# An H3 scan block with a gated linear unit, forward and backward: the first shift's loads, the queue of the h stores, and the transforms of slice 0

## The chip, the cores and the metric

The kernel runs on one core of a Trainium2 chip. The metric is the device time of one execution in microseconds, here the median of eight runs. TensorE (PE) multiplies matrices, VectorE (DVE), ScalarE (ACT) and GpSimd (POOL) work on elements, and SyncE (SP) only issues DMAs; ACT and POOL issue DMAs too. Each engine runs its own list of instructions in order and waits for the others by semaphores.

## The reference

The program computes a block's output and the gradients of its inputs. S is 2048, D is 1024, F is 3584, everything is bf16 at the edges. The core of the forward side:

```python
def _A_ref(q, k, v, shift_k, ssm_k, ssm_D):      # q is the layer-normed x
    k_shift = sum over t of k_pad[:, t:t + S, :] * shift_k[:, ks - 1 - t]     # 4 taps
    kv = k_shift * v
    y = irfft(rfft(kv, padded to 2S) * rfft(ssm_k, padded to 2S))[:S]
    return q * (y + kv * ssm_D)

def _B_ref(x, w_gate, w_up, w_down):
    return ((x @ w_gate) * (x @ w_up)) @ w_down

xn = _layernorm(A_q)
out = A_q + _A_ref(xn, ...) * silu(_B_ref(xn, ...))
```

The shortened sums stand for the padded loops and the einsums of the original. The outputs are `out` and nine gradients from a vjp with a given output gradient.

## The kernel before

The time has five stretches. A layer norm of the 16 blocks of 128 rows comes first (0 to about 57 us). The forward stage (to about 547 us) multiplies the normed rows with 14 slabs of 256 columns of gate and up weights, and beside it runs the long convolution. Then come the product with w_down and the gate (to about 740 us), the backward products with the backward convolution beside them, and last dx with the layer norm's gradient.

A gate/up *unit* is `gu_unit`: four blocks (one or two in the first units) of one slab. Each block is a *group* of eight 128x512 matmuls into `psg` (L622), evicted by ACT to `gut` (L624). After the unit, VectorE multiplies the halves to `hN` (L632), which is stored to Hd by POOL. Five groups later PE transposes hN into a PSUM tile `tr` (L642), ACT copies it to `hT` (L643, two buffers), and it is stored to HTd. Units are counted below in the order of their hN.

The convolution works on slices of 128 channels, two to a `shift`. A shift (L667) forms kv from the shifted k and v with eight VectorE operations over 128x4096 each. Its inputs are k from `KSLd` in two halves and v, all loaded by POOL (`cld`) in `load_kv`, and the taps `Wbc`. A forward transform of kv or of the filter h goes through PE against sine and cosine tables `TF` into `psF` (L234, two PSUM buffers), is copied by ACT to `SP` (L256 or L294, two buffers), and is finished on VectorE. There are two forms. The four-residue form (`fwd4_half`) splits the sequence less on VectorE and multiplies both table halves on PE, 32 matmuls of 128x256; the eight-residue form (`fwd8_half`, `fwd8`) does one more butterfly step on VectorE, 16 matmuls. The list EIGHT says which slices take the second form. After that come the product of the spectra, an inverse transform on VectorE (`inv_dft`) and on PE (`inv_rows`, into `psY`), and `yf`, stored to YFd.

`angles` on POOL makes the integer angles of the tables, `mask_angles` on VectorE reduces them, `build_tables` on ACT takes the sines, `turn_tables` transposes them on PE. `Dz` is a row of ssm_D that enters the h transform by a small matmul (L239).

What sets the order: instructions are recorded in program order and a scheduler places them on the engines. `tc.issue_after(x)` keeps what is inside behind x. Once `PIN[0]` is set, VectorE's operations in `tt` and `stt` keep their program order. `conv` is a generator; each `next` records one piece and yields its weight. `pump` runs it up to a share of its total weight, and `tick`, called after each gate/up group, raises that share. `st` issues on POOL, `ld` on SP, `sta` on ACT. In the first stretch the loop over `xs` records the layer norms and first units, and inside it the pieces of set-up work, among them `next(conv)`, which loads one half of k and v.

Of the kernel before, what the change touches and what calls it, by code (L numbers as in the profile page):

```python
# [10 lines left out]
ACT = mybir.ActivationFunctionType  # L11
# [8 lines left out]
def build_kernel(  # L20
# [11 lines left out]
    nc = tc.nc  # L32
    P = 128
    _, S, D = A_q.shape
# [5 lines left out]
    SLW = 256  # L40
    NSL = F // SLW
    EPS = 1e-5
    WSC = 2.0 / 2048.0
# [14 lines left out]
    ADD, SUB, MUL = ALU.add, ALU.subtract, ALU.mult  # L58

    def ld(out, in_):  # L60
        return nc.sync.dma_start(out=out, in_=in_)
# [3 lines left out]
    def st(out, in_):  # L65
        ins = nc.gpsimd.dma_start(out=out, in_=in_)
        if PINQ[0]:
            tc.keep_in_program_order(ins)
        return ins
# [41 lines left out]
    HTd = [[dram.tile([n, S // 2], BF16, name=f"HTd{i}{n}") for n in (24 * P, 4 * P)] for i in range(2)]  # L111
# [43 lines left out]
    def angles(tg):  # L155

        E = nc.gpsimd
        tcol = tg.tile([P, 8], I32, name="tcol")
        E.iota(tcol[:], pattern=[[1, 8]], base=0, channel_multiplier=8)
        f2 = tg.tile([P, P], I32, name="f2")  # L160
        E.iota(f2[:], pattern=[[4, P]], base=1, channel_multiplier=0)
        m = tg.tile([P, 8, P], I32, name="m")
        ins = E.tensor_tensor(m[:], f2[:].unsqueeze(1).to_broadcast([P, 8, P]),
                              tcol[:].unsqueeze(2).to_broadcast([P, 8, P]), ALU.mult)
        mm = tg.tile([P, 8, P], I32, name="mm1")
        E.iota(mm[:], pattern=[[512, 8], [0, P]], base=0, channel_multiplier=0)
        E.tensor_tensor(mm[:], m[:], mm[:], ADD)
        return (m, mm), ins

    def mask_angles(ang):  # L170

        for x in ang:
            V.tensor_single_scalar(x[:], x[:], 4095, ALU.bitwise_and)

# [10 lines left out]
    def turn_tables(psp):  # L185

        for j in range(2):
            for rq in range(2):
                ps = psp.tile([P, 4, 2, P], BF16, name="psY")
                for i in range(4):  # L190
                    for k in range(2):
                        nc.tensor.transpose(ps[:, i, k, :], T4[j][:, 4 * rq + i, k, :], ident[:])
                nc.scalar.copy(out=TI[:, j, 4 * rq:4 * rq + 4], in_=ps[:])
                yield
# [16 lines left out]
    def tt(o, a, b, op):  # L211
        pinned(V.tensor_tensor(o, a, b, op))  # L212
# [306 lines left out]
    Dz = kst.tile([P, D], BF16, name="Dz")  # L519
# [17 lines left out]
    tr_ln, act_copy = [None], [None]  # L537
# [56 lines left out]
    nop = lambda: None  # L594
# [3 lines left out]
    def defer(fn):  # L598
        later.append([0, fn])
# [10 lines left out]
    def gu_unit(sl, b0, n, w, tick):  # L610

        if n == 4:
            gut = fg.tile([P, 2, 4, SLW], BF16, name="gut")
            hN = fg.tile([P, 4, SLW], BF16, name="hN", bufs=3)
        else:
            gut = lnp.tile([P, 2, 2, SLW], BF16, name="gut_s", bufs=6)
            hN = lnp.tile([P, 2, SLW], BF16, name="hN_s", bufs=6)
        for i in range(n):
            q, qi = divmod(b0 + i, 4)
            ps = ps_gu.tile([P, 512], F32, name="psg")  # L620
            for dc in range(DC):
                gu_mm[0] = nc.tensor.matmul(ps[:], XNT[q][:, dc, qi * P:(qi + 1) * P],  # L622
                                            w[:, dc].rearrange("p a f -> p (a f)"), start=(dc == 0), stop=(dc == DC - 1))
            nc.scalar.copy(out=gut[:, :, i], in_=ps[:].rearrange("p (a f) -> p a f", a=2))  # L624
            flush(5)
            hn[0]()
            hn[0] = nop
            tick()
        sta(GUd[sl, b0 // 8][:, :, b0 % 8:b0 % 8 + n], gut[:, :, 0:n])

        def multiply():
            tt(hN[:, 0:n], gut[:, 0, 0:n], gut[:, 1, 0:n], MUL)  # L632
            st(Hd[sl][:, b0:b0 + n, :], hN[:, 0:n])
            defer(turn)
        hn[0] = multiply

        def turn():
            hT = fg.tile([P, 2, 4, P], BF16, name="hT")
            ps = ps_tr.tile([P, 2, 4, P], BF16, name="tr")
            for a in range(2):  # L640
                for i in range(n):
                    nc.tensor.transpose(ps[:, a, i, :], hN[:, i, a * P:(a + 1) * P], ident[:])  # L642
            nc.scalar.copy(out=hT[:, :, 0:n], in_=ps[:, :, 0:n])  # L643
            fr, so = sl % 12 * SLW, b0 % 8 * P
            st(HTd[b0 // 8][sl // 12][fr:fr + SLW, so:so + n * P].rearrange("(a f) s -> f a s", f=P),
               hT[:, :, 0:n].rearrange("f a i s -> f a (i s)"))

    h_out = []
    EIGHT = (7,)
    SHIFT_W = 8 * 2.3  # L650

    def conv_forward():
# [33 lines left out]
        def h_rows(ds):  # L686
            hrow = S_.pop(("h", ds))
            hx = cs.tile([P, NB, P], BF16, name="hx")
            pe_us[0] += 0.95
            for c in range(2):  # L690
                ps = ps_tr.tile([P, 8, P], BF16, name="tr")
                with tc.issue_after(tr_ln[0].ins):
                    nc.tensor.transpose(ps[:, 0, :], hrow[:, c, :, 0], ident[:])
                for r in range(1, 8):
                    nc.tensor.transpose(ps[:, r, :], hrow[:, c, :, r], ident[:])
                nc.scalar.activation(hx[:, 8 * c:8 * c + 8, :], ps[:], ACT.Copy, scale=WSC)
            h_out.append(ds)
            if ds + 1 < 8:
                load_h(ds + 1)
            S_["hx"] = hx  # L700
# [24 lines left out]
        def half(ds, x, i, first=None):  # L725
            if ds not in EIGHT:
                return fwd4_half(x, i, cs, ps_cv, first)
# [4 lines left out]
        def transform(ds, sp, X, C, ahead, step):  # L732

            if ds in EIGHT:
                W = fwd4_buf(cs)[:].rearrange("p a b c x -> p (a b c) x")
# [20 lines left out]

        yield from shift(0)
        PIN[0] = True
        yield 4.0
        h_rows(0)  # L760
        tl = turn_tables(ps_y)
        sp = [half(0, kvs(0), i) for i in range(2)]
        for ds in range(8):
            yield 0.5
            if ds % 2 == 1 and ds < 7:
                with tc.issue_after(S_["kst"].ins):
                    for c in range(2):
# [8 lines left out]
            next(tl, None)  # L776
            room = cs.tile([P, 4, 256], F32, name="room", tag="hx")[:] if ds in EIGHT else None
            yield from transform(ds, sph, HX, room, lambda i: h_rows(ds + 1) if i == 1 and ds < 7 and ds not in EIGHT else None,
                                 lambda: next(tl, None))
            if ds < 7 and ds in EIGHT:  # L780
                h_rows(ds + 1)
# [15 lines left out]
        for _ in tl:  # L797
# [5 lines left out]
    F_TOTAL = 4 * SHIFT_W + 6.0 + 8 * (0.5 + FWD4_W + 1.3 + PROD_W + INV_W) + 10.0 - 0.95 * 8 * (4 * 1.75 + 0.95 + 4 * 0.9)  # L803
    F_TOTAL += len(EIGHT) * 2 * (FWD8_W - 9.6 + 0.95 * 1.75) - 2.0
    conv = conv_forward()
    chunks = [(0, 1), (1, 1), (2, 2), (4, 4), (8, 4), (12, 4)]
    xs = [(b0, n, u8((4, 6, 7)[b0 // 4 - 1], a=4) if n == 4 else lnp.tile([P, n, D], BF16, name=f"x{b0}")[:])
          for (b0, n) in chunks]
    for c in xs[0:2]:
        ln_load(*c)  # L810
    slabs = [load_slab(0, nc.sync)[0]]
# [9 lines left out]
    ang, ang_ins = angles(tg)  # L821
# [4 lines left out]
    last, root, xst = layer_norm(*xs[0])  # L826
    xsts = [xst]
    for i, (b0, n, x4) in enumerate(xs):
        if i + 1 < len(xs):
            with tc.issue_after(last.ins):  # L830
                last, root, xst = layer_norm(*xs[i + 1])
            xsts.append(xst)
        if i == 1:
            with tc.issue_after(xsts[-1].ins):
                for j in range(4):
                    turn_taps(j)
                nc.gpsimd.tensor_single_scalar(Dz[0:1, :], Dz[0:1, :], WSC, MUL)
            with tc.issue_after(last.ins):
                mask_angles(ang)
        if i == 2:  # L840
            with tc.issue_after(xsts[-1].ins):
                spread_taps()
        if i in (3, 4):
            with tc.issue_after(xsts[4].ins):
                next(conv)
        for i_, sl in ([(0, 0)], [(1, 0), (0, 1), (1, 1)], [(2, 0), (2, 1)], [(3, 0), (3, 1)], [(4, 0)], [(5, 0)])[i]:
            gu_unit(sl, *xs[i_][0:2], slabs[sl], nop)
        if i == len(xs) - 1:
            with tc.issue_after(root.ins):
                build_tables(tg, ang)  # L850
    st(RSd.rearrange("(c u r) -> u c r", c=2, u=P), RSTD[:].rearrange("u (c r) -> u c r", c=2))
    st(RSTN[:], RSd.rearrange("(b p) -> p b", p=P))
# [2 lines left out]
    ps_st.release()  # L855
    ps_cv = pool("ps_cv", 2, space=PSUM)
    pump, drain = make_pump(conv, F_TOTAL)
    cnt = [0]
    NT = 24 * 8.0 + 4

    def tick():
        cnt[0] += 1
        pump((SHIFT_W + (F_TOTAL - SHIFT_W) * (cnt[0] + 5) / (NT + 2)) / F_TOTAL)

    pump(SHIFT_W / F_TOTAL)
    for i_, t_ in ((4, nop), (5, tick)):
        gu_unit(1, *xs[i_][0:2], slabs[1], t_)
    for sl in range(2, NSL - 2):
        w, wld = load_slab(sl, nc.sync)
        if sl in (2, 4, 6):  # L870
# [5 lines left out]
    slabs = [load_slab(NSL - 2, nc.sync)[0]]  # L876
# [678 lines left out]
```

## Time and profile before

| | us |
|---|---|
| median of 8 runs (1956.44 to 1966.72) | 1958.92 |
| the profiled execution | 1958.46 |
| its span, first to last instruction | 1956.7 |
| PE busy | 1919.2 |
| VectorE busy | 1518.9 |
| ACT busy | 637.6 |
| POOL busy | 358.7 |
| mean granted TensorE clock | 0.997 |

Busy time is the union of an engine's instructions; what is missing to the span is time in which it stood still. Line numbers (L622) are those of the kernel before. A timeline row has the start in us from the span's start, the length in us, the engine, the line, the operation, the tiles written and read, the shape, the count of merged instructions, and in brackets the idle time before it and what ended that. L212 is the helper `tt`, L66 is `st` and L61 is `ld`, so their rows are told apart by their tiles. A tile name such as U stands for several buffers.

### The profile page before, as it was taken

To read this page: it belongs to the slowest core of one execution; us is meant where nothing else is said; L and a number is where in the kernel's file an instruction comes from. 1 tells how busy PE (TensorE), PEld (TensorE's weight loads), DVE (VectorE), ACT (ScalarE), POOL (GpSimd) and SP (SyncE) were. 2 spreads that over 40 slices of the span, in tenths; PEclk is the share of its full clock that TensorE was granted. 3 is DMA by queue.
4 is the path that set the end of the run, shared out by engine and by line. 5 is a ranking of instruction groups with operands and counts; after the bars stand their busy time and mean duration, and the time that the engine had idled before them with its cause. 6 is when DMAs were issued, how large, how long until landed. Compare 5 with 4: busy or idle time off the path is not lost. (4 is left out here: it accounts for less than half of the span.)

```text
span 1956.7 us, 27285 instructions
## 1 busy us (share of the span) xinstructions
PE 1919.2 (98%) x10909; PEld 1040.6 (53%) x11043; DVE 1518.9 (78%) x1674; ACT 637.6 (33%) x940; POOL 358.7 (18%) x516
## 2 busy tenths in 40 slices
PE   8899999999999999999999999999999999999999
PEld 4555555555444446666566666664444444444444
DVE  8799999899726555888799899999996403778663
ACT  4755555555432224333222222222222102011122
POOL 6222212111112221000113122021121101112111
PEclk8999999999999999999999999999999999999999
DMA  8767757647799989556778779666796999898993
GB/s 280 256 236 268 260 206 248 231 179 233 269 286 304 279 267 325 183 202 214 247 245 269 264 225 277 206 240 217 195 270 161 164 211 213 142 212 168 181 222 116
DMA packets 445279, 448.62 MB, mean 229 GB/s; under 512 B 265876, under 2 KB 362200, under 8 KB 430688
## 3 DMA queue, kind: packets, MB, share of 16 engines
q1 hardware_dynamic: 384832, 232.86, 45.9%
q0 software_dynamic: 44000, 184.65, 28.5%
q10 hardware_dynamic: 16320, 29.36, 4.1%
q8 instruction: 86, 1.41, 0.3%
q14 instruction: 41, 0.34, 0.1%
HBM read 198.20 MB, written 189.84 MB: 198 GB/s over the span
## 5 line engine op out<-in xcount | busy, mean ns | idle before, releaser
L622 PE MATMUL psg<-wslab,U 128*128 128x512 bf16 x1734 | 401.6, 380 | 8.8 <-ACT gut L624 4.0
L1265 PE MATMUL psb<-U,U 128*128 128x512 bf16 x1792 | 397.4, 379 | 0.0
L1392 PE MATMUL psx<-U,dgut 128*128 128x512 bf16 x1507 | 331.5, 379 | 3.8 <-DMA dgut<-DGd 1.6
L1392 PEld LDWEIGHTS <-dgut 128*128 128x128 bf16 x1792 | 175.2, 98 | 214.2 <-DMA dgut<-DGd 2.4
L1265 PEld LDWEIGHTS <-U 128*128 128x128 bf16 x1792 | 175.3, 98 | 197.5
L622 PEld LDWEIGHTS <-U 128*128 128x128 bf16 x1792 | 173.4, 98 | 193.8 <-issue 7.0
L1248 PE MATMUL psb<-wdt,U 128*128 128x256 bf16 x1792 | 205.3, 273 | 1.1 <-DMA U<-XNd 1.1
L1248 PEld LDWEIGHTS <-U 128*128 128x128 bf16 x1792 | 175.2, 98 | 32.0 <-issue 1.4
L624 ACT CAST gut<-psg 128x512 bf16<-128x512 f32 x216 | 126.3, 587 | 187.7 <-PE psg L622 168.7
L1341 PE MATMUL psb<-U,U 128*128 128x512 bf16 x813 | 179.6, 379 | 1.0
L1117 PE MATMUL psbm<-U,ht 128*128 128x512 bf16 x768 | 168.9, 379 | 0.8
L1270 ACT CAST wb<-psb 128x512 bf16<-128x512 f32 x112 | 65.5, 585 | 311.2 <-PE psb L1265 293.0
L212 DVE TENSOR_TENSOR W<-W 128x1024 f32<-128x1024 f32 (+1 forms) x150 | 151.3, 1027 | 3.2
L1341 PEld LDWEIGHTS <-U 128*128 128x128 bf16 x896 | 87.5, 98 | 105.4 <-issue 1.0
L1117 PEld LDWEIGHTS <-ht 128*128 128x128 bf16 x784 | 76.6, 98 | 91.8
L1424 ACT ACTIVATE dx_t<-dxn 128x1024 bf16<-128x1024 f32 x15 | 15.9, 1057 | 323.8 <-DVE dxn L212 314.7
L1250 ACT CAST dht<-psb 128x512 bf16<-128x512 f32 x112 | 65.6, 586 | 121.4 <-PE psb L1248 120.2
L212 DVE TENSOR_TENSOR U<-U,dht 128x2048 bf16<-128x2048 bf16 x56 | 68.3, 1221 | 46.0 <-ACT dht L1250 45.8
L1098 DVE SCALAR_TENSOR_TENSOR dkp<-dkT,kT 128x1024 bf16<-128x1024 bf16 (+2 forms) x64 | 78.3, 1224 | 22.6 <-DMA dkT<-DKSHd 20.7
L212 DVE TENSOR_TENSOR dxn<-psx,dxna_t 128x1024 f32<-128x1024 f32 x15 | 18.3, 1222 | 91.6 <-PE psx L1392 85.3
L1371 ACT CAST wbs<-psb 128x512 bf16<-128x512 f32 x52 | 30.4, 585 | 148.2 <-PE psb L1341 142.8
L212 DVE TENSOR_TENSOR W<-SP 128x1024 f32<-128x1024 f32 x64 | 74.3, 1220 | 4.6 <-ACT SP L256 3.8
(246 smaller groups left out, 2385.1 us busy)
## 6 DMA issues: line engine op xcount, KB each, us to landing
U<-GUd SPq DMA_DIRECT2D x28, 1024.0 KB, 7.9
DGd<-U SPq DMA_DIRECT2D x28, 1024.0 KB, 4.9
GUd<-gut ACTq DMA_DIRECT2D x54, 512.0 KB, 6.4
out_dram<-wb SPq DMA_DIRECT2D x112, 128.0 KB, 4.1
U<-Hd SPq DMA_DIRECT2D x14, 1024.0 KB, 5.8
Hd<-hN POOLq DMA_DIRECT2D x54, 256.0 KB, 4.3
HTd<-hT POOLq DMA_DIRECT2D x54, 256.0 KB, 4.1
ht<-HTd SPq DMA_DIRECT2D x7, 1536.0 KB, 9.5
```

The lines of the kernel that those rows point to most:

```text
L212: pinned(V.tensor_tensor(o, a, b, op))
L622: gu_mm[0] = nc.tensor.matmul(ps[:], XNT[q][:, dc, qi * P:(qi + 1) * P], w[:, dc].rearrange("p a f -> p (a f)"), start=(dc == 0), stop=(dc ...
L624: nc.scalar.copy(out=gut[:, :, i], in_=ps[:].rearrange("p (a f) -> p a f", a=2))
L1098: ins = V.scalar_tensor_tensor(prod[:].rearrange("p r d -> p (r d)")[:, lo:H], dkT[:, 0, lo:H], 1.0, kT[:, 0, 13 + m + lo:13 + m + H], op0 ...
L1117: nc.tensor.matmul(ps[:, dh * 512:(dh + 1) * 512], ht(fc)[:, i * P:(i + 1) * P], WD[fc // 4][:, fc % 4, dh * 512:(dh + 1) * 512], start=(f ...
L1248: nc.tensor.matmul(ps[:, x * SLW:(x + 1) * SLW], DBMT[2 * hf + g][:, dc, (b % 4) * P:(b % 4 + 1) * P], wdt[:, dc, :], start=(dc == 0), sto ...
L1250: nc.scalar.copy(out=dht[:, 2 * e:2 * e + 2].rearrange("p b f -> p (b f)"), in_=ps[:])
L1265: nc.tensor.matmul(ps[:], XN[b // 4][:, b % 4, dc * P:(dc + 1) * P], dgus[b // 8][:, :, b % 8], start=(b == 0), stop=(b == NB - 1))
L1270: nc.scalar.copy(out=wb[:, dc % 2].rearrange("p a f -> p (a f)"), in_=ps[:])
L1341: nc.tensor.matmul(ps, h[:, b, f * P:(f + 1) * P], DBM[b // 4][:, b % 4, dh * 512:(dh + 1) * 512], start=(b == 0), stop=(b == NB - 1))
L1371: nc.scalar.copy(out=wbs[:, dh * 512:(dh + 1) * 512], in_=ps[:])
L1392: nc.tensor.matmul(ps[:, dh * 512:(dh + 1) * 512], t[n][:, f, i * P:(i + 1) * P], WGU[n][:, f, dh * 512:(dh + 1) * 512], start=(n == 0 and ...
```

## The change

Six things are done.

The two calls of `next(conv)` that load the halves of k and v for the first shift both stand in the loop's fourth round (i == 3), behind the store of the fifth chunk's rows (xsts[4]); before, the second stood in the fifth round.

The store of hT to HTd is issued by SP (`ld`) and not by POOL (`st`).

EIGHT gains slice 0, so its two forward transforms take the eight-residue form. For a slice in EIGHT other than the last, `h_rows` of the next slice is recorded after the h transform and not inside it.

The integer addition that makes the second set of angles moves from POOL to VectorE, and together with both masks it is recorded after the last layer norm, before the tables; before, the addition was on POOL at the start and the masks on VectorE after the third layer norm.

The scaling of Dz moves from POOL to ACT, behind the last copy of the layer norm's transposes at that point (act_copy) in the fifth round.

The weights and ticks are shifted: a weight of 4.0 ahead of `h_rows(0)` becomes 3.9 and 0.1, ticks are also counted in the first unit after the loop, and the count starts at -6 with one pump of its own at -2.

```diff
         mm = tg.tile([P, 8, P], I32, name="mm1")
         E.iota(mm[:], pattern=[[512, 8], [0, P]], base=0, channel_multiplier=0)
-        E.tensor_tensor(mm[:], m[:], mm[:], ADD)
         return (m, mm), ins
     def mask_angles(ang):
+        m, mm = ang
+        tt(mm[:], m[:], mm[:], ADD)
         for x in ang:
             V.tensor_single_scalar(x[:], x[:], 4095, ALU.bitwise_and)
...
             fr, so = sl % 12 * SLW, b0 % 8 * P
-            st(HTd[b0 // 8][sl // 12][fr:fr + SLW, so:so + n * P].rearrange("(a f) s -> f a s", f=P),
+            ld(HTd[b0 // 8][sl // 12][fr:fr + SLW, so:so + n * P].rearrange("(a f) s -> f a s", f=P),
                hT[:, :, 0:n].rearrange("f a i s -> f a (i s)"))
...
-    EIGHT = (7,)
+    EIGHT = (0, 7)
...
         yield from shift(0)
         PIN[0] = True
-        yield 4.0
+        yield 3.9
         h_rows(0)
+        yield 0.1
...
                 for j in range(4):
                     turn_taps(j)
-                nc.gpsimd.tensor_single_scalar(Dz[0:1, :], Dz[0:1, :], WSC, MUL)
-            with tc.issue_after(last.ins):
-                mask_angles(ang)
...
-        if i in (3, 4):
+        if i == 3:
             with tc.issue_after(xsts[4].ins):
-                next(conv)
+                for _ in range(2):
+                    next(conv)
+        if i == 4:
+            with tc.issue_after(act_copy[0].ins):
+                nc.scalar.activation(Dz[0:1, :], Dz[0:1, :], ACT.Copy, scale=WSC)
...
         if i == len(xs) - 1:
-            with tc.issue_after(root.ins):
+            with tc.issue_after(root.ins), tc.issue_after(last.ins):
+                mask_angles(ang)
                 build_tables(tg, ang)
...
-    cnt = [0]
-    NT = 24 * 8.0 + 4
+    cnt = [-6]
+    NT = 24 * 8.0 + 2
     def tick():
         cnt[0] += 1
-        pump((SHIFT_W + (F_TOTAL - SHIFT_W) * (cnt[0] + 5) / (NT + 2)) / F_TOTAL)
+        if cnt[0] == -2:
+            pump((SHIFT_W + 3.95) / F_TOTAL)
+        if cnt[0] >= 0:
+            pump((SHIFT_W + (F_TOTAL - SHIFT_W) * (cnt[0] + 5) / (NT + 2)) / F_TOTAL)
     pump(SHIFT_W / F_TOTAL)
-    for i_, t_ in ((4, nop), (5, tick)):
-        gu_unit(1, *xs[i_][0:2], slabs[1], t_)
+    for i_ in (4, 5):
+        gu_unit(1, *xs[i_][0:2], slabs[1], tick)
```

## The prediction

> **What bounds the kernel now.** I read the page's busy times first, then TensorE's waits by stretch, then the timeline around the one long wait, then the granted clock there, and last what VectorE and SP do until the forward stage ends.
>
> ```profile
> PE 1919.2 (98%) x10909; PEld 1040.6 (53%) x11043; DVE 1518.9 (78%) x1674; ACT 637.6 (33%) x940; POOL 358.7 (18%) x516
> ```
>
> TensorE is the bound. A change pays if it removes matmuls or one of the 37.5 us (1956.7 - 1919.2) in which PE stands. The waits of PE between 81 and 150 us:
>
> ```profile
> PE psF L234 <- DVE kv L212: 4.6, 1, 4.6
> PE psF L234 <- ACT SP L256: 1.7, 2, 1.4
> ```
>
> The first is the longest wait of PE in the run. Its history, from the timeline (start, length, instruction, idle before it):
>
> ```profile
> 44.93 0.53 POOL L66 DMA_DIRECT2D k<-KSLd  x1
> 58.24 0.55 POOL L66 DMA_DIRECT2D k<-KSLd  x1
> 67.19 2.29 DVE L212 TENSOR_TENSOR U<-k,Wbc 128x4096 bf16<-128x4096 bf16 x1 [10.24 <-DMA k<-KSLd]
> 84.30 2.29 DVE L212 TENSOR_TENSOR kv<-U,U 128x4096 bf16<-128x4096 bf16 x1
> 86.64 3.27 PE L234 MATMUL psF<-kv,TF 128*128 128x256 bf16 x16 [4.61 <-DVE kv L212]
> 90.24 1.99 PE L234 MATMUL psF<-kv,TF 128*128 128x256 bf16 x16
> ```
>
> POOL issues the second half of k 13.3 us after the first. It lands 8.9 us later, VectorE has then stood idle for 10.24 us, the shift ends at 86.6, and PE has waited since 82.03. The next sixteen matmuls take 3.27 us where the sixteen after them take 1.99. The granted clock is the reason (stretch, PE busy, and near the end of the row PEclk):
>
> ```profile
> 28.96:32.37 3.41, 1.54 (x14) 0.76 (x12) 3.19 (x12) 3.35 (x6) 1.48 (x4) 1.00 0.25 82
> 32.37:35.78 3.41, 3.16 (x25) 2.85 (x27) 2.40 (x4) 2.29 (x4) 1.54 (x3) 0.50 0.65 250
> 83.57:86.98 3.41, 0.34 (x4) 0.30 (x4) 3.38 (x3) 0.00 (x0) 0.56 (x1) 1.00 0.92 369
> 86.98:90.40 3.42, 3.42 (x21) 2.61 (x19) 0.21 (x1) 1.46 (x2) 1.09 (x2) 0.50 0.79 255
> ```
>
> After a stretch with little PE work the clock is 0.50 for 3.42 us. That half lost clock costs 3.42 x 0.5 = 1.7 us more.
>
> VectorE has room in the forward stage. These are its waits from 60 to 512 us, then SP's longest issue and the last large wait of that stage:
>
> ```profile
> DVE hN L212 <- ACT gut L624: 13.5, 8, 5.3
> ...
> 219.34 13.55 SPq L61 DMA_DIRECT2D KSLd<-in_A_k_dram  x1
> ...
> 515.40 1.01 ACT L643 COPY hT<-tr 128x1024 bf16<-128x1024 bf16 x1 [3.57 <-DMA HTd<-hT]
> ...
> 516.96 13.97 PE L622 MATMUL psg<-wslab,U 128*128 128x512 bf16 x63 [1.93 <-ACT gut L624]
> ```
>
> In those 13.5 us VectorE is ahead of PE and waits for the next evicted gate/up group.
>
> **Part A, the first shift sooner.** Both halves of k and v are issued after the same XNd store: the second k follows the first k (0.53) and two v loads (1.51), so it goes at 44.93 + 2.04 = 46.97 and not at 58.24; with the same 8.9 us it lands near 55.9. On POOL it passes one Hd store (held back 2 us, nobody waits for it) and the last XNd store, which is not ready before 55.33. Wbc, issued at 41.38, landed in 6.9. Then VectorE decides. Its last layer-norm row ends at 55.03. The two masks (0.69 + 0.67) leave the layer-norm chain, so take 53.7. In the built order there follow the integer add, two U copies (1.39), one hN (0.69) and the masks (1.36). No VectorE row shows an integer add of 1024: the POOL row has 2.37, the integer mask 0.69, the f32 add of that size 1.22. I take 1.22, the nearest in engine and form. The shift starts near 53.7 + 1.22 + 1.39 + 0.69 + 1.36 = 58.4, 8.8 sooner, and kv is done near 86.6 - 8.8 = 77.8. PE reaches its first kv matmul about where it did: the built order puts 4 gate/up matmuls and 8 transposes more ahead of it and 6 table transposes fewer (+1.0), and part C takes about as much off, so 82.0. That leaves 4.2 us of cover; without it each us of lateness comes back on PE. Gain: 4.6 + 1.7 = 6.3.
>
> The Trainium skill, TensorE: Matmul & The Clock Gate, section HAM oscillation, asks for no idle gap above about 3.4 us. Here the first clock row above differs: a gap of 1.66 us at 29.55, in a stretch with 1.54 of 3.41 us busy, was followed by 0.50 as well. By the page a leftover wait of 2 us would keep the full clock, by the row it may not.
>
> **Part B, eight residues for slice 0.** The build has 33 matmuls fewer: each of two forward transforms goes from 32 to 16 of 128x256, and one Dz matmul goes. Sixteen such take 1.75 us from start to start (120.69 to the next work at 122.44), 0.109 each. Gain: 33 x 0.109 = 3.6, on PE, where nothing hides it.
>
> Its price on VectorE: a four-residue transform took 9.2 us (100.37 to 109.58); the eight-residue one of slice 7 ran from 483.52 to 502.45, less two hN (1.21) and a 1.81 wait, 15.9. Twice the difference is 13.4 us. ACT has as many copies as before.
>
> **Part C, the layer-norm stretch.** PE waits there 1.66, 0.32 and 0.64 us for L575. VectorE is 1.36 sooner. Against it the Dz scaling (one ACT row of about 1.03, as hx) stands ahead of an eviction, near where PE already waits 0.57 for ACT at 59.03, and the sine now waits for the masks. I take a gain of 1.0; bounds are 2.4 (all three waits gone, masks not missed) and a loss of 1.0.
>
> **Part D, PE against ACT inside slice 0.** The eight tiles of the two transforms now hold 0.44 us of matmuls each, with two PSUM buffers and an ACT copy of 1.02. Between them stand 17 gate/up matmuls (0.216 each, 3.7). PE has 8 x 0.44 + 3.7 = 7.2, ACT 8 x 1.02 + 2 x 0.59 = 9.3. The difference, 2.1, is the upper bound, zero the lower (the first copies overlap what precedes); the four-residue slice lost 0.3 twice here. I take a loss of 1.0.
>
> **Part E, VectorE later on.** First sums: before at 90.99; now PE at 82.0, then the hT copy and two SP copies (3 x 1.02 + 0.2), 85.3, which is 5.7 sooner. Unit 56's hN ran at 511.29 with PE waiting 0.2 for it. By there VectorE has 13.4 us more, less 2.45 of product rows (1.23 + 1.22) that now follow this hN, so 10.95; being later, it spends its 13.5 us of waits first: 511.29 - 5.7 + 10.95 - 13.5 = 503.0, 8.3 sooner. PE would like to be 6.3 + 3.6 + 1.0 - 1.0 = 9.9 sooner. So VectorE holds it back by 1.6. Lower bound zero.
>
> **Part F, h stores on SP.** 60 stores of at most 0.25 MB leave POOL, about 0.71 us of issue each, and join SP. Behind a store that waits for its hT copy stand the next slab load and k copy; a slab load has a whole slab (about 29 us of PE) before it is needed. In the built order each slab has its four stores, in pairs, between its loads, where the copies fall in time anyway, so SP is never parked for long. hT has two buffers, so a store may be about 10 us late (14.7 us for two units, less a landing of 4.1) before ACT stands. I take zero. Upper gain 1.9 (the wait at 515, where a store took 7 us to land behind other POOL stores); the loss is the third rival. Other edits (the tick shift, the POOL add and scale taken off) cost nothing of their own: POOL is 18% busy.
>
> The Trainium skill, Perfetto Trace Analysis, section DMA Optimizations, advises one issuing engine for inputs and another for outputs, which speaks against this part. It gives no price; no row before shows SP held by a store.
>
> **Sum.** -6.3 - 3.6 - 1.0 + 1.0 + 1.6 = -8.3 us. The profiled execution took 1958.46 (span 1956.7 and 1.76 around it), 0.46 below the median of 1958.92. It would become 1950.2, the median 1950.6. From about 500 us on the built order of PE is unchanged, so nothing is given back later.
>
> **Rivals.** *VectorE sets the pace and the change is slower.* The place is unit 56. If the order keeps the 13.5 us of waits, because each hN stands right after its eviction, VectorE is there at 511.29 - 5.7 + 10.95 = 516.5, 5.2 late, and PE with it: 1964.1. It is slower than before as soon as less than 5.2 of the 13.5 are recovered. For: VectorE was 95% busy from 300 to 500 us. Against: an engine that is late does not wait for what is already there. Chance 0.13, of which 0.05 ends slower.
>
> *The first shift is not sooner.* If k's halves, with XNd and v ahead of them, take until 64 or later, kv lands past 83 and wait or clock stay. Then B alone is left: 1955.3. For: DMA was 0.84 busy from 50 to 75. Against: the first half took the same 8 to 9 us to land in that traffic. Chance 0.09.
>
> *SP is blocked.* A k copy's issue once held SP for 13.55 us. With a landing of 4.1 that passes 14.7 and stops ACT for about 3 us, and at 515 a wait of 3.57 on ACT cost PE 1.93. Three k copies: 5.8 given back, 1956.4. Against: the other two issues took 1.48 and 1.76. Chance 0.10.
>
> **Numbers.** The forecast has 0.68. Its own ends: with C at 2.4, D and E at zero and F's 1.9 the gain is 14.2 (1944.7); with C at -1.0 and D at 2.1 it is 5.2 (1953.7). The range runs from 1945.5 to 1957.0, leaving out the slow end of the first rival and the extreme of the forecast. About 0.2% (3.9 us) can be told from no change. Faster: 0.68 and about a third of the others, 0.78; slower by more than that 0.07; 0.15 between.
>
> **What would show it.** the kv product starting near 75.5 and no PE wait for it, full clock from 83 to 91; 33 fewer PE rows; short PE waits on SP copies near 84 to 92; first forward sums near 85; VectorE's waits for gut below 5 us until 512 and PE waiting a little for hN near unit 56; SP's stores issued within 2 us of their hT copies. Wrong if PE still waits over 2 us for kv, if PE waits over 5 us in total for hN, or if ACT waits for HTd more than once or twice.

## The result, and the profile after

The changed kernel takes 1947.39 us (median of 11 runs, 1945.01 to 1953.32) against 1959.04 for the kernel before, run beside it on the same chip: a ratio of 0.9938, 95% interval 0.9923 to 0.9953. That is 11.7 us less; the forecast was 8.3. The profiled execution took 1949.76 us with a span of 1948.0, so that in the traces the change is worth 8.7, from a run 2.4 above its own median.

The medians of the kernel before moved from 1956.2 to 1959.0 between the calls, so results are given below as ratios to the kernel before of the same call; 0.0010 is 2.0 us. Line numbers after are one higher than before (L213 is `tt`, L623 the gate/up matmul, L644 the hT copy); more where the text says so.

The busy times, from the page of after:

```profile
PE 1913.1 (98%) x10873; PEld 1035.3 (53%) x11010; DVE 1530.6 (79%) x1699; ACT 638.2 (33%) x941; POOL 310.5 (16%) x454
```

PE has 6.1 us less, VectorE 11.7 more. Now the timeline of after, the rows that answer to the history of the long wait (start, length, instruction, idle before it):

```profile
45.42 0.53 POOL L66 DMA_DIRECT2D k<-KSLd  x1
47.46 0.55 POOL L66 DMA_DIRECT2D k<-KSLd  x1
...
60.95 2.29 DVE L213 TENSOR_TENSOR U<-k,Wbc 128x4096 bf16<-128x4096 bf16 x1
...
78.06 2.29 DVE L213 TENSOR_TENSOR kv<-U,U 128x4096 bf16<-128x4096 bf16 x1
...
85.14 1.04 PE L235 MATMUL psF<-kv,TF 128*128 128x256 bf16 x8
...
88.26 4.63 DVE L213 TENSOR_TENSOR W<-SP 128x1024 f32<-128x1024 f32 x4 [6.74 <-ACT SP L295]
```

The second half of k goes out 2 us after the first, the shift no longer waits for it, kv is done at 80.35 and PE reaches its first kv matmul 4.8 us later without a wait. VectorE then stands 6.74 us until the first copies arrive. The waits of PE from 100 to 560 us:

```profile
PE psF L235 <- DVE kv L213: 1.9, 2, 1.1
PE tr L694 <- ACT hx L697: 1.6, 2, 1.4
PE psg L623 <- ACT gut L625: 1.4, 1, 1.4
PE tr L643 <- DVE hN L213: 1.4, 1, 1.4
...
PE psF L235 <- ACT SP L257: 1.0, 3, 0.3
```

Before, gut cost 3.5 us there and SP 2.1; now these are 1.4 and 1.0, and kv and hN, which VectorE makes, cost 3.3. VectorE itself has used up its slack (waits of VectorE from 60 to 512 us, where before had 13.5 for gut):

```profile
DVE hN L213 <- ACT gut L625: 0.8, 2, 0.5
```

What the prediction did not have lies earlier, in the layer norm. Timeline and granted clock (stretch, busy times, near the end of the row PEclk, DMA share, GB/s) of after:

```profile
40.30 0.37 ACT L644 COPY hT<-tr 128x256 bf16<-128x256 bf16 x1 [4.52 <-DMA HTd<-hT]
40.72 0.27 PE L643 MATMUL tr<-ident,hN_s 128*128 128x128 bf16 x2 [3.73 <-ACT hT L644]
...
41.58 0.18 DVE L559 RECIPROCAL rr<-r__595 128x4 f32<-128x4 f32 x1 [3.00 <-ACT r__595 L555]
```

```profile
36.91:40.32 3.41, 0.08 (x1) 0.00 (x0) 1.60 (x8) 0.02 (x1) 0.26 (x1) 1.00 1.03 376
...
42.05:45.46 3.41, 3.41 (x15) 1.63 (x13) 3.20 (x11) 2.04 (x3) 0.57 (x2) 0.50 0.19 53
...
86.98:90.40 3.42, 3.31 (x24) 2.06 (x22) 2.14 (x2) 3.42 (x5) 0.00 (x0) 1.00 1.03 350
```

The hT copy on ACT waits 4.52 us until an earlier store of hT has landed and its buffer is free; PE waits for ACT (3.73), the layer norm's square root stands behind it on ACT (3.00 on VectorE), and half a clock follows for 3.41 us (1.7 lost). At 87 us, where before had its half clock, there is none.

### The profile page after: what moved, and what is told of

It reads as the page before. It is cut to its first block, busy times and chain, and to the rows that moved or that the text cites. A ratio compares the mean times of both kernels' runs of the same rounds, so it can differ in the third digit from the quotient of the medians.

```text
span 1948.0 us, 27225 instructions
## 1 busy us (share of the span) xinstructions
PE 1913.1 (98%) x10873; PEld 1035.3 (53%) x11010; DVE 1530.6 (79%) x1699; ACT 638.2 (33%) x941; POOL 310.5 (16%) x454
## 4 chain that ended last, share of the span: by engine, by line
PE 88%; DVE 6%; DMA 2%; issue 2%; ACT 1%; SPq 0%; another core or an unknown queue 0%; POOL 0%; ACTq 0%; DVEq 0%
PE psb L1272 20%; PE psx L1399 20%; PE psg L623 13%; PE psb L1255 10%; PE psbm L1124 10%; PE psb L1348 9%; PE psF L235 2%; DVE W L213 2%; PE psY L447 1%; PE tr L643 1%; DVE U L213 1%; DMA HTd<-hT 1%; DVE KX L213 1%; PE psY L1053 1%; PE psY L436 1%
## 5 line engine op out<-in xcount | busy, mean ns | idle before, releaser
L623 PE MATMUL psg<-wslab,U 128*128 128x512 bf16 x1731 | 405.1, 381 | 7.8 <-DMA wslab<-in_B_w_gate_dram 1.6
L623 PEld LDWEIGHTS <-U 128*128 128x128 bf16 x1792 | 173.2, 98 | 190.0 <-issue 4.7
L213 DVE TENSOR_TENSOR W<-W 128x1024 f32<-128x1024 f32 (+1 forms) x156 | 156.5, 1021 | 3.4
L213 DVE TENSOR_TENSOR U<-U,dht 128x2048 bf16<-128x2048 bf16 x56 | 68.3, 1221 | 46.1 <-ACT dht L1257 46.0
L213 DVE TENSOR_TENSOR dxn<-psx,dxna_t 128x1024 f32<-128x1024 f32 x15 | 18.3, 1222 | 103.3 <-PE psx L1399 99.8
L213 DVE TENSOR_TENSOR W<-SP 128x1024 f32<-128x1024 f32 x64 | 74.1, 1221 | 7.5 <-ACT SP L295 6.7
```

## The experiments

All twelve kernels are told. Where nothing else is said, the edit is made on the changed kernel.

**The h stores back on POOL (part F undone).**

```diff
-            ld(HTd[b0 // 8][sl // 12][fr:fr + SLW, ...
+            st(HTd[b0 // 8][sl // 12][fr:fr + SLW, ...
```

> The changed kernel (median 1947.4) with the h stores back on POOL, the rest as changed. Theory one, the stores on SP cost time in the layer norm: the trace after has PE standing 3.73 us at 36.99 behind the hT copy, which waits for an earlier store of hT to land, then 3.4 us of half clock (1.7 lost). Both go: 1942 to 1945, and no wait of PE over 2 us between 30 and 45 us. Theory two, SP was a gain, because a store from POOL lands late in POOL's traffic (the wait of 3.57 of ACT at 515 before): 1948.5 to 1950.5, with such waits of ACT back between 100 and 560 us. Theory three, the queue does not matter and the wait at 37 us is of the landing in a crowded memory system: 1947.4 within 1.0, and the wait at 37 us stays.

Measured: 1948.81, ratio 0.9961 [0.9944, 0.9978]. The wait of 3.7 us at 37 us is down to 0.5, yet the kernel is not faster than after (0.9938 [0.9923, 0.9953]); the intervals overlap. Theory one does not hold for the kernel as a whole.

**Six hT buffers for the small units, the stores still on SP.** All engines keep their order of instructions.

```diff
-            hT = fg.tile([P, 2, 4, P], BF16, name="hT")
+            hT = (fg.tile([P, 2, 4, P], BF16, name="hT") if n == 4
+                  else lnp.tile([P, 2, 2, P], BF16, name="hT_s", bufs=6))
```

> The changed kernel, with six hT buffers of their own for the units of one and two blocks (two shared ones before); every engine's order of instructions is the same. If the buffer is what ACT waited for at 37 us (a store from SP that had not landed), the wait of 3.73 us of PE goes and the half clock behind it too: the forward stage ends 2 to 5.4 us sooner and the median is 1942 to 1945.5. If ACT only waits for something else that comes at that time (the layer norm's own loads and rows), the gap moves to the next instruction and the median stays at 1947.4 within 1.0.

Measured: 1942.92 (1941.20 to 1943.62), ratio 0.9919 [0.9897, 0.9941], the best of all. The waits of PE from 30 to 60 us in its trace:

```profile
PE tr L587 <- DVE U L576: 1.3, 2, 0.7
PE psg L623 <- ACT gut L625: 0.6, 1, 0.6
```

The wait for hT is gone and no half clock follows. So the stall is the buffer, which comes free when a store has landed. The interval of the ratio overlaps that of after, so the 0.0019 (3.7 us) rests on the trace too. The times themselves do not overlap: the slowest of these six runs (1943.62) is below the fastest of after (1945.01) and below the fastest of a kernel further down that ran beside it and has the stall in its trace (A's recording undone, 1944.71 to 1949.01).

**Four residues for slice 0 again (part B undone).**

```diff
-    EIGHT = (0, 7)
+    EIGHT = (7,)
```

> The changed kernel without slice 0 in EIGHT. PE gets its 33 matmuls back (3.6 us), VectorE loses about 13 us of work. If VectorE now co-limits the forward stage (after, PE waits 0.71 and 1.14 for kv at 198 and 304 us, 1.39 for hN at 504 and 1.45 for gut at 509), these waits go, and the median is 1947.4 + 3.6 - 3.2 = 1947.8, within 1.0. If VectorE had room, part B was worth its 3.6: 1951.0, with the waits of PE as after.

Measured: 1958.40, ratio 1.0003 [0.9988, 1.0018]. Neither value: without B the whole gain is gone, 12.7 us for a part that holds 3.6 us of matmuls. The timeline of this kernel shows where:

```profile
203.83 0.54 POOL L66 DMA_DIRECT2D KFd<-KX  x1 [1.73 <-DVE KX L213]
204.36 0.54 POOL L66 DMA_DIRECT2D k<-KSLd  x1
...
212.42 13.09 SPq L61 DMA_DIRECT2D KSLd<-in_A_k_dram  x1
...
236.61 1.01 ACT L644 COPY hT<-tr 128x1024 bf16<-128x1024 bf16 x1 [6.35 <-DMA HTd<-hT]
...
238.59 3.42 PE L235 MATMUL psF<-kv,TF 128*128 128x256 bf16 x16 [5.03 <-ACT SP L257]
```

The third of the three later copies of k (called the third copy from here on) holds SP for 13.09 us. The h stores behind it go out late, the first at 225.62, where it holds SP for another 5.23. ACT waits 6.35 for a buffer, PE waits 5.03 for ACT's next copy and then runs sixteen matmuls in 3.42 instead of 1.91. This is the mechanism of the prediction's third rival, in a kernel without part B, and from one copy where the rival reckoned with three. After has the copy in 3.05:

```profile
200.39 3.05 SPq L61 DMA_DIRECT2D KSLd<-in_A_k_dram  x1
...
218.38 0.54 POOL L66 DMA_DIRECT2D KFd<-KX  x1 [13.34 <-DVE KX L213]
...
219.51 0.54 POOL L66 DMA_DIRECT2D k<-KSLd  x1
```

With eight residues VectorE is later, and its KFd store goes at 218.38 and not at 203.83; so the loads of k and v, behind KFd on POOL, follow the copy. With four residues they begin 8 us ahead of it. In the traces of all kernels with the copy on SP they begin 8 to 11 us ahead of it with four residues and behind it with eight, and the issue of that copy took:

| slice 0 | kernels with the copy on SP | issue, us |
|---|---|---|
| four residues | before, F alone, A alone, both with B undone (h on SP, h on POOL) | 13.55, 11.56, 12.85, 13.09, 14.39 |
| eight residues | after, B alone, and the five others | 3.05, 0.83, 3.03 to 3.84 |

**The same, with the three later copies of k issued by POOL.** (A variable `h_st` keeps the last Hd store, behind which the copy is placed. PE, VectorE and ACT keep their order of instructions.)

```diff
-        ld(KSLd[dp, 3:3 + S, :]...
+        (ld if dp == 0 else cld)(KSLd[dp, 3:3 + S, :]...
...
-            with tc.issue_after(wld.ins):
+            with tc.issue_after(h_st[0].ins):
```

> The kernel without slice 0 in EIGHT (1958.4, ratio 1.0003), with the three later copies of k issued by POOL and not by SP. If the 13.1 us that the third copy held SP, with h stores queued behind it, made that kernel 8 to 9 us longer than its twin with the stores on POOL (0.9957), SP's stores go out at once, ACT waits for no hT near 230 us, PE's wait of 5.0 and the half clock after it go: a ratio of 0.996 to 0.997. If it is the traffic of the copy itself that delays the stores, whoever issues it: 1.000, with the wait still there.

Measured: 1951.37, ratio 0.9964 [0.9951, 0.9978]. The stall is gone, 7.6 us by the ratios; ACT waits 0.24 us for hT at 229.58. So it needed the copy in SP's list ahead of the h stores. But SP is still held at this place, now by an h store itself:

```profile
215.57 8.23 SPq L61 DMA_DIRECT2D HTd<-hT  x1
```

In these two traces what SP issued next after its slab loads, with the loads of k and v out on POOL, took long, once a copy and once a store; the copy with a store behind it was more than two hT buffers cover, the store alone was not. As POOL issues the copy only at 238.28, this run doesn't exclude that the copy's own traffic delayed the stores. The next one does.

**Parts B and F undone together.** The two edits above (EIGHT and `st`).

> The changed kernel without slice 0 in EIGHT and with the h stores back on POOL: beside the kernel with the h stores on POOL alone (1948.8) it is part B alone, with SP out of it. If the 11 us that leaving slice 0 out cost came from SP (a k copy that took 13.1 us to issue, the h stores behind it, hT late by 6.4 us, PE by 5.0 and a half clock), they go: 1949 if VectorE co-limits with eight residues, 1952.4 if B is worth its full 3.6. If they came from the transforms themselves, 1958 again.

Measured: 1948.67, ratio 0.9957 [0.9943, 0.9972], beside 0.9961 with B. Where the stores are not on SP, a copy of 14.39 us at the same place (209.76) is followed by no wait for hT, and B is worth nothing that the intervals show. From the first kv matmul to the end of the forward stage the traces have 456.4 us without B and 456.3 with it. The waits of PE from 100 to 560 us, first without B, then with it:

```profile
PE psg L623 <- ACT gut L625: 4.0, 2, 2.6
...
PE tr L643 <- DVE hN L213: 0.5, 1, 0.5
...
```

```profile
PE tr L694 <- ACT hx L697: 2.0, 2, 1.8
PE psg L623 <- ACT gut L625: 1.9, 1, 1.9
PE psF L235 <- DVE kv L213: 1.8, 2, 1.1
PE tr L643 <- DVE hN L213: 1.4, 1, 1.4
...
PE psF L235 <- ACT SP L257: 1.0, 3, 0.3
```

The 3.6 us of matmuls come back as waits for kv, hN, hx and SP: 6.2 with B, against 0.5 and 0.2 for hx (in the left-out rows) without it, less 2.1 for gut.

**Part B alone, on the kernel before.** The EIGHT edit there.

> The kernel before with eight residues for slice 0 and nothing else (h stores on POOL). The first shift is as late as before. If VectorE has the room, 33 matmuls go and nothing comes back: a ratio to before of 0.998. If VectorE is late near unit 56 (5 us by the prediction's second rival, where no wait is recovered) the ratio is 1.000 to 1.002, with waits of PE for hN or kv between 190 and 512 us.

Measured: 1954.52, ratio 0.9990 [0.9976, 1.0004]: between the two, 2.0 us, with an interval that takes in both no gain and the full 3.6. PE still waits 1.96 for the first kv, and 3.6 for kv later.

**Part A alone, on the kernel before.** The edit of the diff above, `if i == 3` with two `next(conv)`.

> The kernel before with both halves of k and v recorded in the fourth round and nothing else. By the prediction's term the wait of 4.6 us for kv and the half clock behind it (1.7) go: 6.3 us, a ratio to before of 0.9968. Against it stands the kernel before with the h stores on SP alone, where the second half also went out sooner (47.66) and the first kv matmul came 3.8 us sooner after the first row, but waits of PE for gut grew from 3.5 to 6.6 us: if the sooner start is partly given back so here too, 0.9980 to 0.9990.

Measured: 1951.07, ratio 0.9967 [0.9951, 0.9983], that is 6.5 us against 6.3 predicted. Its timeline:

```profile
45.17 0.55 POOL L66 DMA_DIRECT2D k<-KSLd  x1
55.50 2.29 DVE L212 TENSOR_TENSOR U<-k,Wbc 128x4096 bf16<-128x4096 bf16 x1 [0.32 <-DMA k<-KSLd]
...
80.84 1.91 PE L234 MATMUL psF<-kv,TF 128*128 128x256 bf16 x16
```

No wait for kv, and sixteen matmuls in 1.91, at the full clock.

**Part A's recording undone.**

```diff
-        if i == 3:
+        if i in (3, 4):
             with tc.issue_after(xsts[4].ins):
-                for _ in range(2):
-                    next(conv)
+                next(conv)
```

> The changed kernel with the second half of k and v in the fifth round again, as before. If part A was worth what the prediction said, 6.3 us, the median is 1953.7, with a wait of PE of about 4 us for kv near 82 us and a half clock near 87. If VectorE sets the pace later on as well, its lateness of about 8.8 us is not made up and is seen again as waits for kv or hN: 1955 to 1958. If the load was never what held the first shift, 1947.4 to 1949.

Measured: 1946.98, ratio 0.9941 [0.9919, 0.9963], as after. The edit undid little: POOL, without the h stores, issues the second half of k at 48.48 anyway.

**The second half of k behind the last rows' store.** As above, with `tc.issue_after(xsts[i + 1].ins)`.

> The changed kernel with the second half of k and v behind the last rows' XNd store on POOL, where it goes out near 57 us and not at 47.46 (recording it a round later alone had left it at 48.48). It lands near 66, the first shift starts 5 us later than after's 60.95, kv is done near 85. If part A was worth its 6.3 us here too, 1953.7, with PE waiting 4 us for kv and a half clock after it. If A is covered, because PE itself is late from the layer norm (its first kv matmul is at 85.14 after), there is no wait at kv, and only VectorE's 5 us stay: 1947.4 to 1950.5, with longer waits of PE for kv or hN between 190 and 512 us.

Measured: 1945.97, ratio 0.9940 [0.9922, 0.9957], as after. The load goes out at 53.35 (sooner than expected), VectorE waits 6.38 for it, kv is done at 82.41, PE waits 1.6, and nothing more. Part of the lateness is covered by PE, the rest costs what the row shows.

**Part F alone, on the kernel before.** The `ld` edit.

> The kernel before with the h stores on SP and nothing else. Against: the wait of PE for hT in the layer norm (3.7 us and half a clock of 1.7), and the third k copy, whose issue took 13.55 us near 219 us before, with stores behind it now: PE waits 2 to 5 us there. For: POOL has fewer issues ahead of the second half of k, and may issue it sooner (near 48 and not at 58.24 us), which gives back up to 6.3. Both together: a ratio to before of 0.998 to 1.003. If SP's stores cost nothing, as the prediction had it, and POOL's order moves, 0.997; if nothing moves, 1.000.

Measured: 1953.46, ratio 0.9980 [0.9969, 0.9991], as expected of both effects together: the second half of k goes at 47.66 by itself and the wait for kv is gone, while the third copy holds SP for 11.56, ACT waits 11.5 us in four times for hT, and PE 6.6 in eight for gut (3.5 in four before).

**Part C undone, with the hT buffers of the best kernel.** The masks, the integer add and the Dz scaling go back to where they stood.

> The kernel with more hT buffers in the layer norm (1942.9, ratio 0.9919), with the masks, the integer add and the Dz scaling back where they were before (part C undone). The prediction gave C 1.0 us (bounds 2.4 of gain, 1.0 of loss): 0.9924. From the first statistics row to the last layer-norm row the traces have 51.1 us before, 52.6 with the h stores on SP alone, and 45.8 to 47.0 with C where hT does not stall: if C made that, 4 to 5 us come back, 0.994 to 0.9945.

Measured: 1943.78, ratio 0.9924 [0.9902, 0.9947], against 0.9919 with C. That is the 1.0 us predicted, although the interval alone would allow several us on either side, no gain among them. The layer norm itself, from the first statistics row to VectorE's last row, is shorter in the traces with C. The five traces without it took 49.7 to 52.6 us (49.9 here); those with it and without a stall of hT 45.8 (the best kernel), 46.4, 47.0 and 49.1. But C then puts the integer add and the masks between the layer norm and the first shift, which starts at 53.70 in the best kernel and at 56.07 here. So the 4 to 5 us do not show in the time.

**The best kernel with the copies of k on POOL.** The two edits of the copies, on the kernel with six hT buffers.

> The kernel with more hT buffers in the layer norm (1942.9, ratio 0.9919), with the three later copies of k issued by POOL and not by SP. In that kernel ACT waits for hT only near 540 us, where no copy of k runs. So nothing is to be gained: 0.9919 within 0.0010. If the copies had held SP in some of its executions, 0.990; if they hold POOL's queue instead (Hd, k and v, KFd behind them), 0.993 to 0.996.

Measured: 1946.88 (1944.76 to 1956.23), ratio 0.9935 [0.9910, 0.9960]. It is not better, and the interval does not tell it from 0.9919. Two of eight runs took 1956; the profiled one is of these and shows one wait of 3.9 us for gut, and a wait of 3.2 for a load (A<-DYd) in the backward stage.

## Why the prediction was right

The sign, the place and the largest term were right; the forecast was 3.4 us short of the medians and 0.4 of the profiled executions.

Part of that closeness is luck. Summed by stretch, PE's waits before and after were these:

| us of the span | before | after |
|---|---|---|
| 0 to 24 | 6.3 | 6.7 |
| 24 to 81 | 3.7 | 5.6 |
| 81 to 100 | 4.9 | 0.2 |
| 100 to 560 | 7.4 | 8.6 |
| from 560 | 4.1 | 2.5 |

The third row is part A. The second row has the stall of hT, 3.7 us that no term of the sum had, with a half clock (1.7) behind it. It was mostly paid for by things that the sum did not have either: a half clock of 1.7 at 32 us that only before shows, 0.8 us of waits for ACT's evictions and copies that went, and a wait of 1.6 near 1885 us.

**A** was predicted at 6.3 and measured alone at 6.5. Its steps hold: the load at 47.46 (46.97), the integer add 1.22 us on VectorE as chosen, cover of 4.8 (4.2). The shift started at 60.95 and not at 58.4, because VectorE's last layer-norm row was late by the hT stall. What was not seen is that F moves the same load: alone it puts it at 47.66. In the change the two are redundant, so that undoing A's recording costs nothing.

**B, D and E** were predicted at -3.6 + 1.0 + 1.6 = -1.0. The matmuls went (33, PE's busy time is 6.1 lower with the half clocks in it). The row of D is 0.21 us. E's mechanism was right and its size short: VectorE recovered 12.7 of its 13.5 us of waits, so the first rival fell, and PE waits 1.4 for hN near unit 56 (1.6 predicted), but also 1.9 for kv at shifts two and three, which the sum did not have. Measured, B is worth 2.0 alone and 0 beside A and C, each within 3 to 5 us, which takes in the predicted 1.0. The step that failed is that the sum treated B and F as independent: with the stores on SP, B decides whether the third copy of k holds SP for 3 us or for 13, and is worth 12.7 us, of which the copy's stall is 7.6.

**F** was taken as zero with the third rival at a chance of 0.10. In the change it did not come, but the rival is real and needs only four residues in slice 0. The prediction read the 13.55 us from the trace before, but did not ask what sets it, nor what the later VectorE would do to it. "SP is never parked for long" was read from the built order, which has no durations: an h store between 468 and 482 us, behind loads of w_down and HTd on SP itself, held SP for 8.34 us in after, and for 7.20 to 13.53 in the other kernels with the stores on SP. The Trainium skill, Perfetto Trace Analysis, section DMA Optimizations, advises separate engines for issuing inputs and outputs; here the price of not doing so is, in the kernel with four residues, the 5.03 and the half clock above, and at that place none in after, where the copy is short.

The step "a store may be about 10 us late before ACT stands" failed in another place. It was worked out for units of four blocks. In the layer norm the units have one block: two hT copies 1.54 us apart (32.30 and 33.84) filled both buffers, the third was wanted at 35.8 and got its buffer at 40.30, in a stretch with the DMA engines at 1.03. That cost 3.73 and half a clock, which the best kernel gives back.

**C** was predicted at 1.0 and measured at 1.0, within intervals wider than that, so the agreement is not evidence for the size. In after's own trace PE's waits for U between 24 and 81 us are 1.9 where before had 2.9, but the stall lies in the same stretch. (The upper bound of 2.4 is a little short of its own three waits, which sum to 2.62.)

What stays open: where the last 3 us between the traces (8.7) and the medians (11.7) come from, beyond the profiled run of after being 2.4 above its median. The median of the kernel before is part of it: set against its medians of the other calls, 1956.2 to 1958.0, the same 1947.39 is 8.8 to 10.6 less and not 11.7. The wait of 1.64 for dgut near 1885 us is in before and not in after, but the kernel with A alone has 1.2 of it too, so it isn't put down to any part. F's worth beside A, B and C (0.9961 to 0.9938) is not settled either: in the call that ran both, the kernel with A's recording undone, which has F, took 1946.98 and the one without F 1948.81, only 1.8 apart, with runs that overlap. That the loads ahead of it are what lengthens the copy's issue is argued and not shown: it rests on the order in twelve traces, and no run moved those loads by themselves.

## What to carry to other kernels

Before stores go on a queue that also carries large copies and loads, look at the longest issue on that queue in the trace, ask which transfers were issued shortly before it and whether the change moves them; what stands behind it waits as long, and so does the engine that wants the buffer. Count buffers against the shortest spacing of the writers, not the usual one. And undo each part of a change from both ends, because two parts can do the same thing or be worth something only together.

## What the runs showed of the hardware

The third copy of k, DRAM to DRAM and 1 MB, held the issuing queue of SP for 0.83 to 14.39 us. All five issues above 11 us were in traces in which loads of k and v had been issued on POOL in the 8 to 11 us before. It is not the copy alone: of the 60 h stores (at most 0.25 MB) the median in after took 0.36 us of issue, the longest 8.34, and the longest of all kernels 13.53.

A gap of PE does not decide the clock by its length alone. In after, 3.73 us were followed by 3.41 us at 0.50. The same gap in the kernel with the second half of k behind the last rows' store was followed by the full clock. Its PE row and two stretches after it:

```profile
37.67 0.27 PE L643 MATMUL tr<-ident,hN_s 128*128 128x128 bf16 x2 [3.72 <-ACT hT L644]
```

```profile
38.00:40.00 2.00, 2.00 (x11) 0.94 (x10) 1.25 (x7) 2.00 (x5) 0.00 (x0) 1.00 0.53 161
40.00:42.00 2.00, 1.95 (x20) 1.09 (x20) 2.00 (x5) 1.97 (x3) 0.15 (x1) 1.00 0.08 19
```

The Trainium skill, TensorE: Matmul & The Clock Gate, section HAM oscillation, asks for no idle gap above about 3.4 us. After agrees with it; by this row a longer gap need not cost the clock, and by the 1.66 us of the kernel before a shorter one can. Gaps of 1.64 to 1.66 us at the same instruction, in the kernels with A, B and F alone and in the one with C undone, were followed by the full clock, so the half clock at 32 us of before need not be the kernel's.

Before and after also ran at 0.50 for 6.8 us from about 8 us on (3.4 lost). Four traces, the best kernel's among them, have nothing of it. The mean clock of one kernel's runs goes from 1.000 to 0.997 with their times: with the second half of k behind the last rows' store, 1944.89 and 1948.32. So a few us between two single runs need not come from the kernel.
